# Large-cache and output-weight loads from GpSimd's software queue, marked as one packet of eight rows per engine, with SyncE passing landings on

## The chip, the cores and the metric

The kernel runs on one core of one Trainium2 chip. The metric is the device time of one execution in microseconds (us).

## The reference

Two attention decodes for one new token, in bf16, joined at the end:

```python
# A: 32 heads, each with its own cache of 32768 keys of 128 values
scores = einsum("bhqd,bhkd->bhqk", q, k_cache) * Dh ** -0.5
o = einsum("bhqk,bhkd->bhqd", softmax(scores), v_cache)
a = o.reshape(B, Sq, H * Dh) @ wo
# B: 32 query heads on 8 cache heads, the last 4096 keys only; the rest is the same
return concatenate([a, b], axis=-1)
```

A head of A has 8 MB of K and 8 MB of V, so the 32 heads of A make 64 loads of 8 MB. All the input is 570 MB, and each byte is used once.

## The kernel before

B is worked first, in two groups, then a loop over the heads of A. K has a buffer of 1.5 heads (three thirds of 32 KB a partition), V a buffer of one head that the two groups of B's values use before. All large loads stand in SyncE's hardware queue.

```python
def load(self, dst, src, sem, *deps):
    self.op("sp", lambda e: e.dma_start(dst, src).then_inc(sem, 16), *deps)

def load_k(self, g, parts):              # one head's K: 128 partitions x 64 KB
    w = HALF * DH
    src = self.kv_src("k", "A", g)[:, 0, :]
    lo = min(self.k_thirds(g))
    free = [self.free["k"][t] for t in self.k_thirds(g)]
    if parts == 1:
        self.load(self.kbuf[:, w * lo:w * lo + 2 * w], src, self.mark("k", 0), *free)
        ...
    else:                                # the last head: two halves
        for i, t in enumerate(self.k_thirds(g)):
            self.load(self.kbuf[:, w * t:w * t + w], src[...], self.mark("k", i), *free)

def load_v(self, g):
    self.load(self.vbuf[:, :], self.kv_src("v", "A", g)[:, 0, :], self.mark("v", 0), *self.free["v"])
```

In this kernel an operation increments one semaphore only, that of the engine in its `to`. If a second engine waits for it too, or one that is not its `to`, that engine is kept in `pending`, and the next operation of the same engine that has neither a `to` of its own nor an engine waiting for it carries the signal:

```python
for o in ops:
    ...
    if to is None:
        to = next((c for c in users + pending), None)
    ...
    pending = [c for c in dict.fromkeys(pending + users) if c != to]
```

## Time and profile before

| | before |
|---|---|
| time, median of 2 | 1328.95 us |
| span of the profiled run | 1326.9 us |
| DMA rate over the span | 430 GB/s |
| one 64 KB row on its DMA engine (packet records) | 2.422 us |
| an 8 MB load after the other, landing to landing | 19.35 us |
| TensorE, VectorE busy | 73%, 56% |

The slices of the page (the span in 40 parts; DMA is the busy share of the 16 DMA engines in tenths, GB/s what they moved):

```profile
DMA  9999999999999999999999999999999999999998
GB/s 393 431 433 436 432 431 435 437 429 433 441 429 433 435 435 431 433 441 429 433 435 435 431 433 441 427 435 435 433 433 433 437 431 435 435 431 435 433 435 341
```

The queue table (queue, kind: packets, MB, share of the engines' time), and the head of the chain that ended last:

```profile
q1 hardware_dynamic: 13048, 570.44, 99.6%
q8 instruction: 12, 0.20, 0.1%
...
DMA 70%; PE 27%; DVE 1%; issue 0%; SPq 0%; ACT 0%
DMA kbuf<-in_A_k_cache_dram 65%; PE psT L497 23%; PE psS L519 4%; DMA kbuf<-in_B_k_cache_dram 3%; DMA kbuf<-in_A_wo_dram 3%; DVE kt L500 1%; PE psACC L599 0%; SPq L288 0%; DVE oc_A L615 0%; ACT psb L547 0%; DVE tr_in L536 0%; PE psPT L571 0%; ACT ptsb L574 0%; PE psPT L661 0%; PE psG L626 0%
```

The engines that move data are busy from the first slice to the last but one. Eight rows of 64 KB stand on each of 16 engines for one load: 8 x 2.422 = 19.38 us, and the landings are nearly that far apart (19.35 us). So any time that counts is time in which these engines are idle, or the stretch after their last byte.

The timeline at the change from B to A (start, duration, engine, line, operation, out<-in; in brackets how long the engine had been idle and what ended it; SPq is SyncE issuing a load):

```profile
54.49 0.34 SPq L288 DMA_DIRECT2D kbuf<-in_A_k_cache_dram  x1
...
64.15 3.37 PE L599 MATMUL psACC<-vbuf,ptsb 128*16 128x512 bf16 x32 [1.20 <-DMA vbuf<-in_B_v_cache_dram]
...
67.57 0.34 SPq L288 DMA_DIRECT2D vbuf<-in_A_v_cache_dram  x1
...
83.52 5.69 PE L497 MATMUL psT<-ident,kbuf 128*128 128x128 bf16 x64 [13.05 <-DMA kbuf<-in_A_k_cache_dram]
...
94.46 0.33 SPq L288 DMA_DIRECT2D kbuf<-in_A_k_cache_dram  x1
```

K of head 0, K(0) for short, is issued at 54.5 us, behind B's last value load in the same queue. That one lands at 63.7 us, its product runs at 64.2 us, and V(0) is issued at 67.6 us. K(0) is still moving until 83 us, so the queue never runs dry. Later V is issued some 6.5 us before it would.

The end of the timeline:

```profile
1279.59 3.82 PE L497 MATMUL psT<-ident,kbuf 128*128 128x128 bf16 x64
...
1313.35 3.40 PE L674 MATMUL psS<-kbuf,oz_B 128*1 128x512 bf16 x32
...
1317.98 1.37 PE L661 MATMUL psPT<-kbuf,oz_A 128*1 128x256 bf16 x22
1319.87 1.04 PE L661 MATMUL psPT<-kbuf,oz_A 128*1 128x256 bf16 x16 [0.52 <-DMA kbuf<-in_A_wo_dram]
1321.75 0.82 PE L661 MATMUL psPT<-kbuf,oz_A 128*1 128x256 bf16 x12 [0.84 <-DMA kbuf<-in_A_wo_dram]
1323.00 0.60 PE L661 MATMUL psPT<-kbuf,oz_A 128*1 128x256 bf16 x8 [0.43 <-DMA kbuf<-in_A_wo_dram]
1323.96 0.49 PE L661 MATMUL psPT<-kbuf,oz_A 128*1 128x256 bf16 x6 [0.36 <-DMA kbuf<-in_A_wo_dram]
```

The transposes of head 31 (first line) start at 1279.6 us, on the first half of K(31); all of K(31) landed at 1284.2 us. The last products (L661) follow the landings of the output weights piece by piece.

### The profile page before, as it was taken

Reading aid. Unit: us, or ns where it says so; the run is one execution under the profiler, and the core shown is the slowest. Engines: PE = TensorE matmul, PEld = TensorE weight load, DVE = VectorE, ACT = ScalarE, POOL = GpSimd, SP = SyncE. Lnnn points to the kernel's source line nnn. Section 1 sums busy time; section 2 is a strip of 40 time slices with the busy share of each in tenths; the row PEclk is TensorE's granted clock in tenths of the full one; section 3 lists DMA queues with packets and bytes.
Section 4 is the critical chain, followed back from the end, with each engine's and each line's share of the span. In section 5 each row is a group of like instructions: output and inputs, shape, how many; then the busy total and the mean of one; then the engine's idle time right before and its main releaser. Section 6 shows DMA issues by size and latency. Waiting matters only on the chain.

```text
span 1326.9 us, 28821 instructions
## 1 busy us (share of the span) xinstructions
PE 963.9 (73%) x13436; PEld 678.1 (51%) x13436; DVE 749.5 (56%) x1345; ACT 54.8 (4%) x167; POOL 2.3 (0%) x17
## 2 busy tenths in 40 slices
PE   3657678777667877766787777678777767877786
PEld 3544445554444555444465544446554444655453
DVE  3645466665456666545666645566664556666473
ACT  0000000000000000000000000000000000000000
POOL 0000000000000000000000000000000000000000
PEclk9877788887788888778888878888887888888798
DMA  9999999999999999999999999999999999999998
GB/s 393 431 433 436 432 431 435 437 429 433 441 429 433 435 435 431 433 441 429 433 435 435 431 433 441 427 435 435 433 433 433 437 431 435 435 431 435 433 435 341
DMA packets 13351, 570.66 MB, mean 430 GB/s; under 512 B 1812, under 2 KB 1816, under 8 KB 2200
## 3 DMA queue, kind: packets, MB, share of 16 engines
q1 hardware_dynamic: 13048, 570.44, 99.6%
q8 instruction: 12, 0.20, 0.1%
q10 hardware_dynamic: 288, 0.00, 0.0%
q14 instruction: 3, 0.02, 0.0%
HBM read 570.43 MB, written 0.00 MB: 430 GB/s over the span
## 4 chain that ended last, share of the span: by engine, by line
DMA 70%; PE 27%; DVE 1%; issue 0%; SPq 0%; ACT 0%
DMA kbuf<-in_A_k_cache_dram 65%; PE psT L497 23%; PE psS L519 4%; DMA kbuf<-in_B_k_cache_dram 3%; DMA kbuf<-in_A_wo_dram 3%; DVE kt L500 1%; PE psACC L599 0%; SPq L288 0%; DVE oc_A L615 0%; ACT psb L547 0%; DVE tr_in L536 0%; PE psPT L571 0%; ACT ptsb L574 0%; PE psPT L661 0%; PE psG L626 0%
## 5 line engine op out<-in xcount | busy, mean ns | idle before, releaser
L500 DVE COPY kt<-psT 128x1024 bf16<-128x1024 bf16 x1056 | 654.8, 683 | 245.3 <-PE psT L497 243.5
L497 PE MATMUL psT<-ident,kbuf 128*128 128x128 bf16 x8448 | 578.7, 234 | 176.7 <-DMA kbuf<-in_A_k_cache_dram 165.0
L497 PEld LDWEIGHTS psT<-ident,kbuf 128*128 128x128 bf16 x8448 | 539.3, 106 | 268.7 <-DMA kbuf<-in_A_k_cache_dram 173.1
L599 PE MATMUL psACC<-vbuf,ptsb 128*4 128x512 bf16 (+1 forms) x2112 | 182.9, 522 | 23.3 <-ACT ptsb L574 21.3
L519 PE MATMUL psS<-kt,qw 128*32 128x512 bf16 x2048 | 157.6, 385 | 15.4 <-DVE kt L500 15.4
L613 DVE TENSOR_SCALAR oc_A<-psACC,hot_A 128x128 f32<-128x128 f32 x32 | 11.2, 350 | 247.7 <-PE psG L626 247.7
L599 PEld LDWEIGHTS psACC<-vbuf,ptsb 128*4 128x4 bf16 (+1 forms) x2112 | 59.0, 110 | 137.8 <-issue 87.6
L547 ACT ACTIVATE psb<-psS,nb_A 128x512 bf16<-128x512 f32 x32 | 22.0, 687 | 1169.8 <-DVE nb_A L546 1169.8
L519 PEld LDWEIGHTS psS<-kt,qw 128*32 128x32 bf16 x2048 | 34.0, 95 | 57.9 <-DVE kt L500 31.3
L626 PE MATMUL psG<-oc_A,hw 128*32 128x128 f32 (+1 forms) x128 | 19.3, 227 | 52.3 <-DVE oc_A L615 52.3
L626 PEld LDWEIGHTS psG<-oc_A,hw 128*32 128x32 f32 x128 | 11.4, 109 | 62.5 <-DVE oc_A L615 55.0
L571 PE MATMUL psPT<-ident,psb 128*128 128x128 bf16 x136 | 18.0, 274 | 34.0 <-ACT psb L547 34.0
L615 DVE SCALAR_TENSOR_TENSOR oc_A<-psACC,hot_A,oc_A 128x128 f32<-128x128 f32 x96 | 33.7, 351 | 3.4
L536 DVE TENSOR_REDUCE tr_in<-psS 128x1 f32<-128x512 f32 x34 | 23.5, 692 | 17.1 <-PE psS L519 17.1
L571 PEld LDWEIGHTS psPT<-ident,psb 128*128 128x128 bf16 x136 | 10.1, 117 | 37.1 <-ACT psb L547 36.7
L540 PE MATMUL psACC<-rows,tr_in 128*1 128x64 f32 x64 | 8.7, 217 | 25.5 <-DVE tr_in L536 25.5
L574 ACT ACTIVATE ptsb<-psPT 128x512 bf16<-128x512 bf16 x34 | 20.3, 597 | 28.3 <-PE psPT L571 28.3
L540 PEld LDWEIGHTS psACC<-rows,tr_in 128*1 128x1 f32 x64 | 2.7, 81 | 35.1 <-DVE tr_in L536 35.1
L544 PE MATMUL psACC<-mr_A,nscale 1*128 1x1 f32 x64 | 12.1, 256 | 9.7 <-DVE mr_A L543 9.7
L544 PEld LDWEIGHTS psACC<-mr_A,nscale 1*128 1x128 f32 x64 | 9.4, 182 | 15.7 <-DVE mr_A L543 15.7
L546 DVE COPY nb_A<-psACC 128x1 f32<-128x1 f32 x32 | 5.1, 158 | 15.0 <-PE psACC L544 15.0
L543 DVE TENSOR_REDUCE mr_A<-psACC 1x1 f32<-1x64 f32 x32 | 6.8, 213 | 11.7 <-PE psACC L540 11.7
(71 smaller groups left out, 75.0 us busy)
## 6 DMA issues: line engine op xcount, KB each, us to landing
kbuf<-in_B_k_cache_dram SPq DMA_DIRECT2D x2, 4096.0 KB, 32.3
vbuf<-in_B_v_cache_dram SPq DMA_DIRECT2D x2, 4096.0 KB, 23.9
kbuf<-in_A_k_cache_dram SPq DMA_DIRECT2D x2, 4096.0 KB, 22.0
vbuf<-in_B_wq_dram SPq DMA_DIRECT2D x1, 4096.0 KB, 12.3
vbuf<-in_A_wq_dram SPq DMA_DIRECT2D x1, 4096.0 KB, 32.2
kbuf<-in_B_wo_dram SPq DMA_DIRECT2D x2, 2048.0 KB, 33.1
kbuf<-in_A_wo_dram SPq DMA_DIRECT2D x1, 1408.0 KB, 28.5
kbuf<-in_A_wo_dram SPq DMA_DIRECT2D x1, 1024.0 KB, 30.8
```

The lines of the kernel that those rows point to most:

```text
L497: inst = e.transpose(T[:, 128 * k:128 * k + 128], src[:, DH * k:DH * k + DH], self.ident[:, :])
L500: self.copies.append(self.op("dve", lambda v: v.tensor_copy(KT[:, :], T[:, :]), o, to="pe"))
L519: inst = e.matmul(self.S[32 * c:32 * c + 32, :], lhsT=win, rhs=self.kt[(bb + c // 2) % NKT][:, 512 * (c % 2):512 * (c % 2) + 512], start=b ...
L536: o = dve(lambda v: v.reduce_max(tr["in"][:, 0:1], self.S[:, :], axis=AXX), self.sdone, self.k_pool, to="pe" if name == "A" else None)
L540: o = self.op("pe", lambda e: e.matmul(self.ACC[0:1, 0:64], lhsT=tr["in"][:, 0:1], rhs=self.rows64[:, :], start=True, stop=True, skip_grou ...
L544: o = self.op("pe", lambda e: e.matmul(self.ACC[:, 64:65], lhsT=self.nscale[:, :], rhs=t["mr"][0:1, :], start=True, stop=True, skip_group_ ...
L547: self.sread = self.op("act", lambda s: s.activation(out=self.psb[:, :], in_=self.S[:, :], func=ACTF.Exp, bias=t["nb"][:, k:k + 1], scale= ...
L571: inst = e.transpose(PT[:, 128 * jj:128 * jj + 128], self.psb[:, 128 * jj:128 * jj + 128], self.ident[:, :])
L574: self.ptread = self.op("act", lambda s: s.activation(out=self.ptsb[:, :], in_=PT[:, 0:512], func=ACTF.Copy), self.psread, to="pe")
L599: inst = e.matmul(acc[32 * c:32 * c + rows, 0:512], lhsT=lhsT, rhs=rhs, start=begin, stop=end, tile_position=(0, 32 * c), skip_group_check ...
L615: o = self.op("dve", lambda v, src=src, hot=hot: v.scalar_tensor_tensor(out=oc, in0=src, scalar=hot, in1=oc, op0=ALU.mult, op1=ALU.add), p ...
L626: return self.op("pe", lambda e: e.matmul(self.G[0:32, c0 + c:c0 + c2], lhsT=win, rhs=t["oc"][g % 2][:, c:c2], start=False, stop=True, ski ...
```

## The change

The intent: the eight rows that an engine moves for a load as a single packet, from GpSimd's software queue, for the 64 loads of 8 MB and the seven of the output weights. TensorE still waits on the old semaphores; SyncE waits for each landing of a large load and increments them (the output weights increment theirs directly). The loads of B stay on SyncE's queue. K(31) becomes one load. Sixteen tiny loads at the end, and the waits for them, go.

```diff
-    def load(self, dst, src, sem, *deps):
-        self.op("sp", lambda e: e.dma_start(dst, src).then_inc(sem, 16), *deps)
+    def load(self, dst, src, sem, *deps, by="sp"):
+        how = {"single_packet": True} if by == "pool" else {}
+        self.op(by, lambda e: e.dma_start(dst, src, **how).then_inc(sem, 16), *deps)
 ...
-        if parts == 1:
-            self.load(self.kbuf[:, w * lo:w * lo + 2 * w], src, self.mark("k", 0), *free)
-            sem = self.mark("k", 1)
-            self.op("sp", lambda e: e.sem_inc(sem, 16))
-        else:
-            for i, t in enumerate(self.k_thirds(g)):
-                self.load(self.kbuf[:, w * t:w * t + w], src[:, w * (t - lo):w * (t - lo) + w], self.mark("k", i), *free)
+        self.load(self.kbuf[:, w * lo:w * lo + 2 * w], src, self.ksemA, *free, by="pool")
 
     def load_v(self, g):
-        self.load(self.vbuf[:, :], self.kv_src("v", "A", g)[:, 0, :], self.mark("v", 0), *self.free["v"])
+        self.load(self.vbuf[:, :], self.kv_src("v", "A", g)[:, 0, :], self.vsemA, *self.free["v"], by="pool")
+
+    def relay(self, g):
+        for which, sem in (("k", self.ksemA), ("v", self.vsemA)):
+            to = [self.mark(which, i) for i in range(2 if which == "k" else 1)]
+            self.op("sp", lambda e, sem=sem: e.wait_ge(sem, 16 * g + 16))
+            for x in to:
+                self.op("sp", lambda e, x=x: e.sem_inc(x, 16))
 ...
         self.load(self.kbuf[:, off + 512 * a0:off + 512 * a1], src[:, 512 * a0:512 * a1], self.wosem[name][part],
-                  self.free["k"][t])
+                  self.free["k"][t], by="pool")
 ...
             self.load_v(g)
+            self.relay(g)
 ...
-        for i in range(16):
-            self.load(self.marks[0:i + 1, 16 * i:16 * i + 16], self.X["A"]["wo"][0:i + 1, 0:16], self.marksem[i])
         self.emit_spread("A")
         self.emit_proj()
-        for i in range(16):
-            self.op("sp", lambda e, i=i: e.wait_ge(self.marksem[i], 16))
 ...
-        pv = self.op("pe", mm, self.landed("v", 0 if name == "A" else g), self.ptread, self.accread, to="sp")
+        pv = self.op("pe", mm, self.landed("v", 0 if name == "A" else g), self.ptread, self.accread, to="pool" if name == "A" else "sp")
```

More of the change, by code (lines that the diff above doesn't have):

```diff
@@ L279, in alloc @@
         self.vsem = [s(f"vsem{i}") for i in range(2)]
+        self.ksemA = s("ksemA")
+        self.vsemA = s("vsemA")
         self.xsem = {n: s(f"xsem_{n}") for n in self.X}
```

## The prediction

> **What bounds it now.** The DMA engines. The page's slices show DMA at 9 tenths throughout and 430 GB/s; in the packet records each 64 KB cache row takes 2.422 us on its engine, eight rows per engine, and landings of whole 8 MB loads are 19.35 us apart. The chain of waits agrees (65% in the large K loads). By the timeline TensorE idles about 4.7 us a head waiting for K; V is issued about 6.7 us, K about 8 us before the queue would run empty.
>
> **What the change can give.** Packets of 32 KB take 1.215 us, of 64 KB 2.422 us: the fixed part is 8 to 10 ns a packet. If one packet for eight rows drops seven fixed parts of eight, 64 loads x 7 x 9 ns = 4 us, an upper bound (0.3%). Nothing can be 2% faster at the same bytes.
>
> **What it costs.**
> 1. Steady state: GpSimd's issue[...] and the relay[...] fit in 5 to 6 us of slack: 0 us.
> 2. [...](a) the last B value load (SyncE's queue, 9.6 us still to move when K of head 0 is issued at 54.5 us) is stuck behind K of head 0; it lands near 84 us instead of 63.6, V(0) is issued about 20 us later, and the engines idle about 5 us.[...]
> 3. Tail: K of head 31 is one load, not two halves. Its transposes start at its full landing (1284.2 us) rather than at 1279.6 us; TensorE's run to the end is then the longer path, by 3 to 4.5 us.
> 4. The sixteen marker loads go; they landed by 1323.3 us, off the path: 0 us.
>
> Sum: 1329 - 3 + 5 + 12 (weighted down, as the packet may be divisible) + 4. If packets are not held whole, I expect 1327 to 1330; if they are, 1340 to 1348.
>
> Predicted 1338 us, 8 in 10 between 1325 and 1352; faster by over 2%: 0.01; within 2%: 0.9; slower by over 2%: 0.09.
>
> **What would show it.** Right: 8 MB landings still 19.3 us apart in mid-kernel (19.28 if the fixed part goes); a software queue in the DMA table; idle DMA slices only in the first 180 us; TensorE waits for "issue" inside transposes of heads 0 and 1; instruction packets bunched at the loads' borders; B's value load landing after K of head 0; transposes of head 31 starting about 5 us later. Wrong: DMA at 9 tenths from the start, instruction packets at their old times.
>
> **What would make it wrong.** A software queue that streams slower (each 1% costs 13 us)[...], a row still costing its 9 ns inside a packet, or an engine that serves other queues between rows.

1329 - 3 + 5 + 12 + 4 came to 1347 us, and weighted down to the 1338 us predicted. The slack of 5 to 6 us and the 5 us of (a) are estimates from the trace before. The fixed part per packet is an estimate too, from the packet records before: 2 x 1.215 - 2.422 = 0.008 us.

## More of the kernel before

The product with V, whose end frees the V buffer, names its `to` itself. Before, that is SyncE, which issues the loads:

```python
pv = self.op("pe", mm, self.landed("v", 0 if name == "A" else g), self.ptread, self.accread, to="sp")
```

## The result and the profile after

The changed kernel takes 1346.17 us (median of 2 runs, 1345.98 to 1346.36) against 1328.95 us: 17.2 us more. The ratio is 1.013, with a 95% interval of 1.010 to 1.016. A ratio here is the mean time of one kernel's fast runs over that of the other's of the same rounds, so it is not quite the ratio of the medians quoted.

| | before | after |
|---|---|---|
| span of the profiled run | 1326.9 us | 1343.9 us |
| DMA rate over the span | 430 GB/s | 425 GB/s |
| one 64 KB row on its engine | 2.422 us | 2.422 us |
| landing to landing in mid-kernel | 19.35 us | 19.35 us |
| B's last value load, first to last engine done | 61.7 to 63.7 us | 76.2 to 82.9 us |
| K(0), first to last engine done | 81.0 to 83.0 us | 81.0 to 82.9 us |
| V(0), last engine done | 102.4 us | 119.8 us |
| V(31), last engine done | 1303.5 us | 1319.5 us |

The last four rows are read from the 4-byte semaphore packets, 16 to a load. Nearly the whole loss is there between K(0), which lands when it did, and V(0), which lands 17.4 us late. Nothing more is lost in the heads that follow: V(31) is 16.0 us late, a little less, as the first and the last engine are 1.9 us apart there instead of 3.2. The remaining 1.2 us of the loss lie behind it, in the tail.

The slices and the queue table after:

```profile
DMA  9959999999999999999999999999999999999998
GB/s 394 430 209 438 433 435 435 437 437 437 425 427 437 433 433 435 437 435 437 427 427 437 433 435 433 437 435 435 427 429 437 433 435 433 437 431 437 429 429 344
...
q0 software_dynamic: 10160, 545.26, 93.9%
q1 hardware_dynamic: 2408, 25.17, 4.5%
q8 instruction: 12, 0.20, 0.1%
```

One slice, the third, has DMA at 5 tenths and 209 GB/s; all others are full. The busy times by stretch say it more sharply (window, us, then busy us and instructions of PE, PEld, DVE, ACT and POOL, that is TensorE, its weight loads, VectorE, ScalarE and GpSimd; granted clock, DMA share, GB/s), first before, then after:

```profile
82.00:100.00 18.00, 16.48 (x242) 13.85 (x243) 14.86 (x24) 0.00 (x0) 0.00 (x0) 0.84 1.00 431
...
160.00:1240.00 1080.00, 803.20 (x11086) 566.03 (x11086) 624.30 (x1091) 44.44 (x140) 0.00 (x0) 0.84 1.00 434
```

```profile
82.00:100.00 18.00, 13.42 (x172) 9.75 (x173) 9.83 (x20) 0.00 (x0) 0.53 (x1) 0.77 0.18 63
...
160.00:1240.00 1080.00, 800.59 (x11044) 560.95 (x11042) 620.40 (x1088) 44.44 (x140) 29.65 (x56) 0.84 1.00 433
```

Between 82 and 100 us the engines were busy for 0.18 of the time; from 160 to 1240 us they moved 433 GB/s against 434. So the software queue streamed as well here as the hardware queue. From the start of the issue to the first row it took 1.2 us on either where the engines were idle or nearly so: 96.67 to 97.89 us for V(0) from GpSimd's, 0.80 to 2.01 us for the first load of the kernel before and 1338.48 to 1339.71 us for the first store of the output after from SyncE's.

The timeline at the change from B to A, after (POOL is GpSimd issuing a load):

```profile
56.19 0.69 POOL L291 DMA_DIRECT2D kbuf<-in_A_k_cache_dram  x1 [53.26 <-PE psS L520]
...
83.36 3.59 PE L600 MATMUL psACC<-vbuf,ptsb 128*16 128x512 bf16 x32 [19.01 <-DMA vbuf<-in_B_v_cache_dram]
...
86.73 0.27 PE L627 MATMUL psG<-oc_B,hsel_B 128*32 128x1 f32 x2
...
90.89 5.12 PE L498 MATMUL psT<-ident,kbuf 128*128 128x128 bf16 x64 [0.99 <-PEq L216]
...
95.94 0.62 PE L520 MATMUL psS<-kt,qw 128*32 128x512 bf16 x8
...
96.67 0.53 POOL L291 DMA_DIRECT2D vbuf<-in_A_v_cache_dram  x1 [39.79 <-PE psS L520]
...
101.53 0.53 POOL L291 DMA_DIRECT2D kbuf<-in_A_k_cache_dram  x1 [4.33 <-PE psS L520]
```

Here two separate delays show. B's last product waits for its values until 83.4 us instead of 64.2 us. And though that product is over at 87.0 us, V(0) is issued only at 96.7 us. The idle time in the brackets of that line ends with a product of scores, psS at L520, and not with the product that frees the V buffer. The list of GpSimd's waits (engine, tile and line it waited with, what ended the wait: us in all, times, longest) has it as a case by itself:

```profile
POOL vbuf L291 <- PE psACC L600: 631.3, 31, 24.3
POOL kbuf L291 <- PE psS L520: 603.1, 33, 53.3
POOL vbuf L291 <- PE psS L520: 39.8, 1, 39.8
```

Of 32 loads of V, 31 are released by psACC at L600, the product with V, and one by psS. The code above says why: B's products still name SyncE as their `to`. GpSimd, which now waits for them, is left pending. The small products behind them and the transposes signal VectorE, so the first operation that is free to carry the signal is the first product of scores in the loop, after 64 transposes of head 0. It stands in the timeline above at 95.9 us.

What the prediction had expected of whole packets is not there. Between 60 and 83 us the packet records show rows of both queues mixed: in eight of the eleven stretches of 2 us from 60 to 82 us, 13 to 16 rows of 64 KB from GpSimd's queue and 6 to 16 rows of 8 KB from SyncE's. Over all eleven it is 128 rows of 64 KB and 108 of 8 KB. So eight rows that were marked as one packet did not keep the rows of the other queue waiting: the two took turns, nearly row for row. Nor did instruction fetches (the 12 packets of 16 KB on queue 8; that they are TensorE's is the reading of their spacing) hold TensorE up: in the second head they come at 149.5, 156.6 and 164.1 us, 7.1 and 7.5 us apart, as before (130.9, 138.3 and 145.6 us, 7.4 and 7.3 us apart). This spacing alone proves little: the first of the two is 9.6 us in e1_signal and e4_rows below, and 9.7 us in b2_nomarks, which has no load in GpSimd's queue; in head 0 the three fetches come 12.6 and 7.3 us apart after, 7.1 and 12.1 us before. What decides is that no wait of TensorE falls to them: the waits before its matmuls that are put down to "issue" come to 0.2 us in the whole run, the one put down to its sequencer (1.0 us, up to 90.9 us) lies between two fetches, at 63.1 and 96.1 us, and the timeline shows the first 64 transposes of heads 0 and 1 in one piece each.

The end of the timeline after:

```profile
1300.70 6.05 PE L498 MATMUL psT<-ident,kbuf 128*128 128x128 bf16 x64 [4.71 <-SPq L332]
...
1334.69 1.90 PE L675 MATMUL psS<-kbuf,oz_B 128*1 128x512 bf16 x32
...
1337.81 3.66 PE L662 MATMUL psPT<-kbuf,oz_A 128*1 128x256 bf16 x64
```

The transposes of head 31 now wait for all of K(31). The last 64 products run in one piece, 3.66 us, with no wait: the output weights are there by 1339.2 us and TensorE is the one that is late, at 1341.5 us.

### The profile page after: what moved, and what is told of

Its sections match the earlier page's. It is cut to its first block, busy times and chain, and to the rows that moved or that the text cites. A ratio compares the mean times of both kernels' runs of the same rounds, so it can differ in the third digit from the quotient of the medians.

```text
span 1343.9 us, 28861 instructions
## 1 busy us (share of the span) xinstructions
PE 964.2 (72%) x13436; PEld 679.3 (51%) x13436; DVE 749.1 (56%) x1345; ACT 54.8 (4%) x167; POOL 40.0 (3%) x88
## 4 chain that ended last, share of the span: by engine, by line
DMA 64%; PE 27%; DVE 1%; issue 1%; ACT 0%; SPq 0%
DMA kbuf<-in_A_k_cache_dram 64%; PE psT L498 22%; PE psS L520 3%; DVE kt L501 1%; PE psACC L600 0%; PE psPT L662 0%; PE psS L675 0%; DVE oc_A L616 0%; SPq L332 0%; ACT psb L548 0%; DVE tr_in L537 0%; DVE pb L678 0%; ACT ptsb L575 0%; PE psACC L662 0%; PE psG L627 0%
## 5 line engine op out<-in xcount | busy, mean ns | idle before, releaser
L600 PE MATMUL psACC<-vbuf,ptsb 128*4 128x512 bf16 (+1 forms) x2112 | 185.7, 528 | 45.0 <-ACT ptsb L575 21.3
L520 PE MATMUL psS<-kt,qw 128*32 128x512 bf16 x2048 | 157.6, 385 | 15.2 <-DVE kt L501 15.2
L600 PEld LDWEIGHTS psACC<-vbuf,ptsb 128*4 128x4 bf16 (+1 forms) x2112 | 60.5, 111 | 160.6 <-issue 95.8
L520 PEld LDWEIGHTS psS<-kt,qw 128*32 128x32 bf16 x2048 | 34.1, 95 | 57.7 <-DVE kt L501 31.0
L291 POOL DMA_DIRECT2D vbuf<-in_A_v_cache_dram x32 | 16.9, 529 | 671.1 <-PE psACC L600 631.3
L291 POOL DMA_DIRECT2D kbuf<-in_A_k_cache_dram x32 | 17.1, 535 | 586.7 <-PE psS L520 586.7
L545 PE MATMUL psACC<-mr_A,nscale 1*128 1x1 f32 x64 | 12.1, 256 | 9.7 <-DVE mr_A L544 9.7
```

Source lines behind the costliest of these rows:

```text
L291: self.op(by, lambda e: e.dma_start(dst, src, **how).then_inc(sem, 16), *deps)
L520: inst = e.matmul(self.S[32 * c:32 * c + 32, :], lhsT=win, rhs=self.kt[(bb + c // 2) % NKT][:, 512 * (c % 2):512 * (c % 2) + 512], start=b ...
L545: o = self.op("pe", lambda e: e.matmul(self.ACC[:, 64:65], lhsT=self.nscale[:, :], rhs=t["mr"][0:1, :], start=True, stop=True, skip_group_ ...
L600: inst = e.matmul(acc[32 * c:32 * c + rows, 0:512], lhsT=lhsT, rhs=rhs, start=begin, stop=end, tile_position=(0, 32 * c), skip_group_check ...
```

## The experiments

The theory after reading the trace, called "theory" in the expectations: the loss is one idle stretch at the change of queues, in two terms, the late signal and the sharing of the engines by rows, and a small tail. Its rivals: A, that the software queue or the relay costs time on every head; B, that rows marked as one packet hold up other queues. All ten kernels gave correct results. Times are medians, with the fast runs' range, and the kernel before was 1328.90, 1328.97 and 1329.02 us in the three sets.

### e1_signal: B's products signal GpSimd directly

```diff
-        pv = self.op("pe", mm, ..., to="pool" if name == "A" else "sp")
+        pv = self.op("pe", mm, ..., to="pool")
```

> One edit to the changed kernel: the products with B's values signal GpSimd directly, so that the load of V for head 0 need not wait for a signal carried by a later product. Theory (one idle stretch at the change of queues; 9.7 us of it is this late signal, as V(0) was issued at 96.7 us though its last reader ended at 86.9 us): V(0) issued near 87 us, DMA idle from 82.9 to about 88.5 us only, time 1336 to 1337.5 us (9 to 10 us less than the changed kernel's 1346). Rival A (the software queue or the relay costs time on every head): time stays within 2 us of 1346. Rival B (whole 512 KB packets hold up instruction fetches in heads 0 and 1): at most 3 us gained[...].

Measured: 1337.08 us (1336.82 to 1338.63), ratio 1.0061 (1.0044 to 1.0077). GpSimd's timeline, V(0) first, then K of head 1:

```profile
87.22 0.53 POOL L291 DMA_DIRECT2D vbuf<-in_A_v_cache_dram  x1 [30.66 <-PE psACC L600]
102.87 0.53 POOL L291 DMA_DIRECT2D kbuf<-in_A_k_cache_dram  x1 [15.12 <-PE psS L520]
```

V(0) is issued at 87.2 us, and all engines are idle from 83.1 to 88.4 us: 5.3 us, where the changed kernel had 14.0 (82.9 to 97.9 us, but for one instruction fetch). The late signal was 9.1 us of the loss. Rivals A and B as the main cause are out; that neither has a smaller share is left to e6_head0 and e8_all.

### e2_wait: K(0) waits until B's last value load has landed

```diff
-        self.load(self.kbuf[:, w * lo:w * lo + 2 * w], src, self.ksemA, *free, by="pool")
+        first = [(self.vsem[1], 32)] if g == 0 else []
+        self.load(self.kbuf[:, w * lo:w * lo + 2 * w], src, self.ksemA, *first, *free, by="pool")
```

> One other edit to the changed kernel: GpSimd's load of K for head 0 also waits until B's last value load has landed, so that the two queues never share the engines; the late signal stays. Theory: B's value load lands near 63.7 us again, K(0) lands at 85 to 86.5 us, the first product of head 0 that carries the late signal comes near 92 us, V(0) is issued then, idle about 86 to 93.5 us: time 1341 to 1343 us. If the shared engines were the whole of the loss and the signal nothing, it would be 1330 to 1332 us; rival A: 1346 to 1347 us.

Measured: 1342.79 us (1342.49 to 1342.94), ratio 1.0105 (1.0088 to 1.0122). GpSimd's timeline, K(0) first, then V(0):

```profile
64.25 0.69 POOL L291 DMA_DIRECT2D kbuf<-in_A_k_cache_dram  x1 [61.31 <-DMA vbuf<-in_B_v_cache_dram]
92.94 0.53 POOL L291 DMA_DIRECT2D vbuf<-in_A_v_cache_dram  x1 [28.00 <-PE psS L521]
```

B's value load lands at 63.5 us again, and all engines are idle for 2.1 us there. But V(0) still waits for the late signal, until 92.9 us, and the engines idle again from 86.3 to 94.2 us, but for one instruction fetch. So keeping the queues apart alone gains 3.4 us: the second delay hides most of the first one's cure.

### e3_both: both edits together

The two diffs above.

> Both edits together: direct signal, and K(0) waits for B's last value load. Theory: V(0) is issued near 68 us, behind K(0) in the same queue; the engines idle only 1.5 to 2.5 us near 65 us; the rest is the tail, about 1 us: time 1331 to 1333.5 us, and the loss is then all but gone with the software queue, the packets and the relay still in place. Rival A: still 1340 us or more, as 64 loads still go by GpSimd. Rival B: still above 1338 us from instruction fetches held up.

Measured: 1334.37 us (1332.92 to 1335.54), ratio 1.0037 (1.0021 to 1.0054), up to 2 us over what was expected. V(0) is issued at 68.9 us, and the only stretch before the end in which all engines are idle is the one of 2.1 us from 63.4 to 65.5 us. The cost of the wait is more than that, as the first engine is done with B's load at 61.6 us already: K(0) lands at 86.1 us, 3.1 us later than in the kernel before. Against e2_wait, the direct signal is worth 8.4 us here. The rest sits in the tail, as e5_split shows below: the last output weights landed at 1326.2 us, but TensorE ran on to 1331.1 us.

### e4_rows: without the single-packet marking

```diff
-        how = {"single_packet": True} if by == "pool" else {}
+        how = {}
```

> The changed kernel with the single-packet marking taken away, nothing else. Theory from the trace after (8 KB rows of SyncE's queue alternate one for one with 64 KB rows of GpSimd's between 60 and 83 us, so rows and not packets are the unit at which an engine changes queue; a 64 KB row takes 2.422 us either way): time within 1.5 us of 1346, landings 19.35 us apart, B's value load lands near 83 us as before. The prediction's view (512 KB packets held whole, and a fixed part saved per packet): B's value load would land earlier than 83 us by several us, and rows in mid-kernel would take about 9 ns longer, 4 us over the kernel.

Measured: 1347.19 us (1345.83 to 1348.28), ratio 1.0134 (1.0117 to 1.0151), the changed kernel's 1346.17 us within the spread. A row takes 2.422 us and B's value load lands at 83.1 us, both as with the marking. The marking did nothing that these runs can see, neither a gain per row nor a hold on the engines. Whether it made one packet of the eight rows is not shown by any run.

### e5_split: e3_both with K(31) in two halves again

```diff
+        else:                                   # parts == 2: head 31
+            for t, sem in zip(self.k_thirds(g), (self.ksemA, self.ksemB)):
+                self.load(self.kbuf[:, w * t:w * t + w], src[...], sem, self.free["k"][t], by="pool")
 # relay: ksemA passes on to ksem0, ksemB to ksem1 for this head
```

> The kernel of the two edits (direct signal, K(0) waits for B's last value load), and K of head 31 again in two halves, each with its own semaphore and relay. Tail theory: in the run with the two edits TensorE ran without waiting from the landing of K(31), 1287.1 us, to the end and the last output-weight landing, 1326.2 us, was 1.2 us before the product that it could have released; with halves the transposes start some 4 to 5 us earlier against the landing of V(31), the product with V waits for V instead, and the end follows the last landing: 1.5 to 3.5 us less than the kernel of the two edits, 1330.5 to 1333 us. If the tail costs nothing: 1334 us as before this edit.

Measured: 1332.19 us (1332.06 to 1332.58), ratio 1.0025 (1.0011 to 1.0039), 2.2 us less than e3_both. The last products follow the landings piece by piece again. The 3.2 us that are left over the kernel before match the wait for B's load: V(31) lands at 1306.6 us, 3.1 us later than there.

### e6_head0: K(0) and V(0) stay on SyncE's queue

The changed kernel, with `by="sp"` and the old marks for head 0, no relay for it, and K(31) in halves. B's products name SyncE, as in the changed kernel.

> The changed kernel with K and V of head 0 left on SyncE's queue (so the loads of B and of head 0 stand in one row, and the late signal of V(0) does not arise, as the signal goes to SyncE again), and K(31) in halves. 62 of the 64 big loads and the output weights still go by GpSimd as single packets with the relay. Theory: no idle stretch at all before the end; V(0) and K(1) share the engines row by row for some us without loss; time 1328 to 1330 us, as the kernel before. Rival A (a cost on every head[...]): 1333 us or more.

Measured: 1329.09 us (1329.01 to 1329.31), ratio 1.0001 (0.9988 to 1.0015). With 62 of the 64 large loads and the output weights still in the software queue, the large loads still relayed, the whole loss is gone. Rival A is out for the loads of heads 1 to 31. (GpSimd's issue of a load takes 0.53 us in the run after, SyncE's 0.33 us before.)

### b1_one: the kernel before with K(31) in one load

```diff
-            self.load_k(g, 1 if g < NQH - 1 else 2)
+            self.load_k(g, 1)
```

> The kernel before, with K of head 31 as one load instead of two halves and nothing else. Tail theory: 1 to 4 us more than the kernel before, 1330 to 1333 us, from TensorE's last stretch alone. If the tail costs nothing: 1329 us.

Measured: 1331.94 us (1330.17 to 1332.93), ratio 1.0021 (1.0008 to 1.0035): 3.0 us more, from this alone. The start of head 31 and the last products of this run:

```profile
1284.68 5.30 PE L497 MATMUL psT<-ident,kbuf 128*128 128x128 bf16 x64 [4.06 <-DMA kbuf<-in_A_k_cache_dram]
...
1323.80 3.66 PE L661 MATMUL psPT<-kbuf,oz_A 128*1 128x256 bf16 x64
```

The transposes wait 4.1 us for K(31), and the last 64 products run in one piece after all weights have landed.

### b2_nomarks: the kernel before without the sixteen tiny loads

The two loops that the change removes are removed; nothing else.

> The kernel before without its sixteen marker loads and the waits for them. They landed by 1323.3 us, ahead of the last output-weight landing and the output store: within 0.5 us of the kernel before, 1328.4 to 1329.4 us. If they held the end up: 1 us or more faster; if they helped the last landings on their way: slower.

Measured: 1329.27 us (1328.55 to 1329.64), ratio 1.0002 (0.9988 to 1.0015). They cost and give nothing that shows.

### e7_rows8: e1_signal, and K(0) in rows of 8 KB

```diff
+        if g == 0:
+            for i in range(8):
+                self.load(self.kbuf[:, w * lo + 4096 * i:w * lo + 4096 * i + 4096], src[:, 4096 * i:4096 * i + 4096],
+                          self.ksemB if i else self.ksemA, *free, by="pool")
+            return
 # relay of head 0: waits for ksemB >= 16 * 7 too
```

> The changed kernel with the direct signal, and K of head 0 loaded by GpSimd in eight column pieces, so that its rows are 8 KB like those of B's value load ([...]K still starts at 56 us, nothing waits). Theory (an engine takes one row from each queue in turn, so a queue with short rows gets few bytes): now both queues get equal bytes, B's value load lands near 67 to 68 us instead of 83, V(0) is issued near 71 us while K(0) is still moving, and no idle stretch is left: 1331 to 1333.5 us, the rest being the tail. Rival (the turn is a packet of eight rows, the prediction's view): B's value load would get one 8 KB row per 64 KB packet as before and still land near 83 us: 1336 to 1338 us. Rival (one queue has simply priority or SyncE's queue is slow beside the other): 1336 to 1338 us as well.

Measured: 1331.25 us (1330.49 to 1333.31), ratio 1.0021 (1.0007 to 1.0035), 5.8 us less than e1_signal. Lines of its timeline, first one of TensorE, then two of GpSimd:

```profile
68.17 3.56 PE L608 MATMUL psACC<-vbuf,ptsb 128*16 128x512 bf16 x32 [4.47 <-DMA vbuf<-in_B_v_cache_dram]
```

```profile
55.40 4.33 POOL L292 DMA_DIRECT2D kbuf<-in_A_k_cache_dram  x8 [52.47 <-PE psS L528]
72.05 0.53 POOL L292 DMA_DIRECT2D vbuf<-in_A_v_cache_dram  x1 [12.32 <-PE psACC L608]
```

K(0) is issued from 55.4 us on (at 56.2 us in the changed kernel; the eight issues take 4.3 us), and B's value load lands at 67.7 us nevertheless. In the packet records the queues now have 46 to 52 rows of 8 KB each in the 2 us stretches from 60 to 64 us. There is no stretch before the end in which all engines are idle. With 64 KB rows against 8 KB rows, SyncE's queue got 0.9 of 9.3 MB from 60 to 82 us in the run after (108 rows and 128); with equal rows it gets half. So the rival that one queue has priority, or that SyncE's queue is slow beside the other, is out too. That the turn is a row, and not a packet, rests on this run and on the mixed rows of the trace after.

### e8_all: e7_rows8 with K(31) in halves

> The same with K of head 31 in two halves again: all three terms repaired (late signal, row sharing, tail) with every large load on GpSimd's software queue and the relay in place. Theory: 1328.5 to 1330.5 us, the kernel before within half a part in a thousand or so; it can't be faster, as the engines are then busy from the first load to the last. Rival A (a cost of the software queue on every head): above 1332 us.

Measured: 1329.90 us (1329.82 to 1330.06), ratio 1.0007 (0.9993 to 1.0021). All large loads are in the software queue, and the kernel is within 0.9 us of the one before. The interval includes no difference, but the runs do not overlap with those before (1328.62 to 1329.43 us), so a few tenths of a us may be a real cost; what they are is not shown.

No version beats the kernel before. From 2 us to 1323 us there is no pause in which all its DMA engines are idle, and the median 64 KB row took 2.422 us in all ten kernels.

## Why the prediction was right or wrong

The time, 1346.17 us, lies in the predicted range of 1325 to 1352 us, and in the narrower one of 1340 to 1348 us that the prediction gave for packets that are held whole. That agreement is in part luck: the rows were not held together, one term of the sum was not real, and one that was real is not in the sum. The terms as written, 1329 - 3 + 5 + 12 + 4, make 1347 us (1338 us was that figure weighted down); the 12 us for fetches, which did not come, stand there in place of 9.1 us of late signal that were not foreseen.

| term | predicted | measured |
|---|---|---|
| a saving per packet | -3 us | 0: 2.422 us a row before, after and in e4_rows |
| steady state: software issue and relay | 0 | 0: 19.35 us from landing to landing; e6_head0 equals the kernel before |
| B's value load stuck beside K(0) | +5 us | 5.8 us (e1_signal to e7_rows8), by another mechanism |
| late signal for V(0) | not seen | 9.1 us (the changed kernel to e1_signal); 8.4 us (e2_wait to e3_both) |
| stall on instruction fetches | +12 us | 0: waits put down to "issue" are 0.2 us in the whole run, none in heads 0 and 1 |
| tail: K(31) in one load | +3 to 4.5 us | 1.4 us (e7_rows8 to e8_all), 2.2 us (e3_both to e5_split), 3.0 us (b1_one) |
| sixteen tiny loads gone | 0 | 0.3 us, inside the spread (b2_nomarks) |
| left over in e8_all | | 0.9 us, its interval includes 0 |

By the repairs in order, 9.1 + 5.8 + 1.4 + 0.9 = 17.2 us is the loss. Each figure is a difference of two runs in one row, so they must add up; the order matters where delays hide each other, as e2_wait shows with 3.4 us.

The 12 us failed. They were the estimate for TensorE in heads 0 and 1, waiting for instructions that come late behind the large loads. No such wait shows in the trace after (0.2 us of "issue" in the whole run). What the estimate rested on is cut, as no run here shows it; in this kernel the marked load did not keep the other queue's rows out (128 and 108 rows, mixed, from 60 to 82 us).

Step 2(a) named the right load, the landing near 84 us (82.9 measured) and an idle time of about 5 us for it. Its reason, that the load "is stuck behind K of head 0", was wrong: it was served all the time, 108 rows of 8 KB beside 128 of 64 KB from 60 to 82 us. Both readings give nearly the same landing: in the kernel before, the load needed 3.6 us more from 60 us on. At 0.312 us for an 8 KB row (median of the packet records) that is, as an estimate, some eleven rows on the slowest engine against eight of K(0), so that it ended just after K(0) either way. The landing alone does not tell them apart; the mixed rows in the trace after do, and e7_rows8, which changes the rows and leaves eight rows marked together.

The same step said "V(0) is issued about 20 us later". It was 29 us later, 96.7 instead of 67.6 us. The diff shows this: its last line gives the products with V of A the new `to`, and leaves that of B. The prediction took the end of a product for the moment at which the load behind it is released, as it is in the profile before, and did not follow the signal through the code.

The tail was the right mechanism, but its predicted size of 3 to 4.5 us was too large: 1.4 to 3.0 us were measured. TensorE's last stretch did not take equally long in all runs: the product with V of head 31 took 4.83 us at a granted clock of 0.74 in the profile after, and 6.22 us at 0.57 in that of e3_both.

## What to carry to other kernels

When loads move to another engine, follow each release signal to its new reader, above all at the borders between phases: a signal that rides on a later operation cost nothing here while a queue was full (K's release rides on a product of scores in every head, with landings 19.35 us apart), and nearly all its delay, 9.1 of 9.7 us, when the queue ran dry. Two queues that fed the same DMA engines shared them here by rows and not by bytes (128 rows of 64 KB beside 108 of 8 KB); put the load that something waits for first in the same queue, or give the other one rows as short. And a sum that comes out right says little about its terms: check each against its own line of the trace.
